# A three-bank score tile that borrows the side work's PSUM bank, and five P buffers for both shapes

## The chip, the cores and the metric

The kernel runs on one core of a Trainium2 chip. The metric is the device time of one execution in microseconds. TensorE (PE) multiplies matrices into PSUM, which has eight banks; ScalarE (ACT) computes the exponentials; VectorE (DVE) and GpSimd (POOL) do elementwise work; SyncE (SP) issues most transfers.

## The reference, cut to what matters

Two identical layers run over x with 2048 rows and 640 columns. Each has an attention block with 32 heads of 20 dimensions and a token-mixing MLP (2048 to 1536 to 2048, along the rows).

```python
x = A_x
x = x + _A_ref(_layernorm(x), A_wqkv, A_wo)                      # attention
x = x + _B_ref(_layernorm(x), B_w1, B_b1, B_w2, B_b2)            # token MLP
x = x + _A_ref(_layernorm(x), A_wqkv, A_wo)
x = x + _B_ref(_layernorm(x), B_w1, B_b1, B_w2, B_b2)

# inside _A_ref, after q, k, v = split(x @ wqkv), H = 32, Dh = 20
scores = jnp.einsum("bhqd,bhkd->bhqk", q, k) * (Dh ** -0.5)
p = _softmax(scores, axis=-1)
o = jnp.einsum("bhqk,bhkd->bhqd", p, v)
```

Per layer that is 2048 x 2048 scores for each of 32 heads, and one exponential for each score.

## The kernel before, in words

**Units, chunks and tiles.** The scores are computed transposed, keys on the 128 partitions. A unit is a group of four heads, a block of 128 keys and a block of 512 queries; it has four chunks, one per head, each 128 keys by 512 queries and as wide as one PSUM bank. A layer has 512 units, 2048 chunks. The loop over t at the end of `attention` goes through score tiles: `take_acts(t)` gathers the next chunks, three where t is even and two where it is odd, `emit_S(t)` (L754) writes the score products of all of them into the tile, and `emit_exp(t)` (L812) has ScalarE turn the whole tile into bf16 probabilities P with one instruction (L818). `emit_PV(n)` (L1418, product at L1440) multiplies the four chunks of a unit with the values and adds them up in the bank `acc`.

**PSUM.** The eight banks are the three-bank score tile, the two-bank score tile, `Dt`, `acc` and `misc`. `misc` is the side work's bank. Side work (fills) are the products that aren't attention itself: projections of queries, keys and values (L1279, L1310), transposes (L1334), the output projection (L1169, L1207) and parts of the token MLP (L1120, L1827). Each group of products fills `misc` and is then evacuated, mostly by VectorE. In the early phase of a layer, before all rows are normalized and projected, `Dt` serves side work too; `feed_ended` closes that phase, opens the pools in the dictionary `late` and takes `Dt` out of the side work's banks.

**Chunks on VectorE.** `ve_admit` (L546) is called once per score tile. Where `Dt` is free and VectorE's backlog is under 7 us, it gives one chunk of a later unit to VectorE: its scores go to `Dt`, and VectorE and GpSimd compute the exponential from bits and a polynomial (L588, L629, L634, L653, L655; L689, L706 on GpSimd). The result is a tile `Pd`.

**P buffers.** P tiles come from two pools of `PT_BUFS` = 3 buffers, one for tiles of three chunks and one for tiles of two. As the shapes alternate, tile t uses the buffer that tile t - 6 had, and ScalarE's write waits until PE has read all of that tile.

**Order of work.** The kernel plans its own order when it is built: PE, DVE, ACT and GpSimd each get a fixed sequence. Clocks for them (`pem`, `dvm`, `acm`) go forward by costs written at the top (`ACT_US`, `WAVE` = 0.2155 us for four products of 512 columns side by side, `ACT_TO_PE` = 0.052 us), and each step asks the clocks what is due. `exp_end[t]` is when ScalarE is planned to finish tile t; scores of tile t + 2 may be written then. `slot_work` (L1496) fills PE's time while an exp runs: a product with the values (`pv_next`, L1459; it is forced once its last tile is `PV_LATE` = 4 tiles back), else side work, else a product with zeros that changes nothing (`zeros`, L775, L807). Side work goes ahead of a waiting product with the values until that is `HOLD` = 3 tiles back. The core of the loop is this:

```python
if not paired and t + 1 not in S_tiles and take_acts(t + 1):
    emit_S(t + 1)
while t - 2 * CFG["PT_BUFS"] in P_tiles:
    slot_work(t, pem["t"] + 0.6, True)
emit_exp(t)
until = exp_end[t] + ACT_TO_PE
while slot_work(t, until):
    ...
```

`P_tiles` holds the tiles that have chunks still to be multiplied. `misc` and `Dbank` (for `Dt`) are objects of the class `Bank`, with `free` as the planned time from which the bank may be used. `next_fill(now)` (L1369) gives the first piece of side work that is ready by then.

Of the kernel before, what the change touches and what calls it, by code (L numbers as in the profile page):

```python
# [12 lines left out]
BF16 = mybir.dt.bfloat16  # L13
F32 = mybir.dt.float32
# [20 lines left out]

CFG = dict(
    KQ_AHEAD=1,
    PT_BUFS=3,
    A0_LAG=2,
    VE_BACKLOG=7.0,  # L40
    VE_MARGIN=3.0,
    VE_LEAST=4,
    PV_LATE=4,
    FILL_ROOM=-0.12,
# [11 lines left out]
ACT_TO_PE = 0.052  # L56
# [16 lines left out]

HOLD = 3
WARM_WAVES = 14
LOG2E = 1.4426950408889634
LN2 = 0.6931471805599453
FIX = 65536.0
# [7 lines left out]
def kernel(  # L86
# [13 lines left out]
    S = A_x.shape[1]  # L100
# [58 lines left out]
    nc.gpsimd.memset(zr[:], 1.0)  # L159
    q_scale = SCALE * LOG2E * FIX  # L160
    x1lp = ctx.enter_context(tc.tile_pool(name="x1lp", bufs=1))
# [12 lines left out]
    def load_w1l():  # L174
        for sti in range(TAIL):
            after_vector(nc.sync.dma_start(out=w1l_view[:, sti, :],
                                           in_=B_w1[(NT - TAIL + sti) * 128:(NT - TAIL + sti + 1) * 128, :]))
# [58 lines left out]

    def open_p_scope(st, stack):
        st.ntmp = stack.enter_context(tc.tile_pool(name=f"ntmp{st.layer}", bufs=1))
        st.ptp = {w: stack.enter_context(tc.tile_pool(name=f"ptp{w}_{st.layer}", bufs=CFG["PT_BUFS"])) for w in (3, 2)}

    def get_QT(st, qb):
        if qb not in st.QTq:
# [3 lines left out]
    def attention(st, x_in_ap, x_mid, uacc_l, feed, feed_stack):  # L246
# [5 lines left out]
        pp = {}  # L252

        def open_psum():
            for name in ("s3", "s2", "dt", "acc", "misc"):
                pp[name] = p1.enter_context(tc.tile_pool(name=f"ps_{name}_{layer}", bufs=1, space=PSUM, reuse_waits="tile"))

        def s_tile(w):
            return pp[f"s{w}"].tile([128, w, 512], F32, name="S")
        ntmp, ptp = st.ntmp, st.ptp  # L260
        p1.enter_context(tc.manual_schedule(engines={nc.vector.engine, nc.scalar.engine, nc.gpsimd.engine}))
        late, ve = {}, {}
# [22 lines left out]
        S_tiles, P_tiles = {}, {}  # L285
        in_attention = [True]

        pem = dict(t=0.0, mode=None)
        dvm = dict(t=0.0, over=DVE_OVER, next=DVE_NEXT, procs=[])
        acm = dict(t=feed.act_free, over=0.0, next=0.06, procs=[])  # L290
# [6 lines left out]
        class Bank:  # L297
            def __init__(self, alloc):
                self.alloc, self.free = alloc, 0.0
        misc = Bank(lambda: pp["misc"].tile([128, 512], F32, name="misc"))  # L300
        Dbank = Bank(lambda: pp["dt"].tile([128, 512], F32, name="Dt"))
        banks = [misc, Dbank]
        spare = [Bank(lambda w=w: s_tile(w)[:, 0, :]) for w in (2, 3)]
# [134 lines left out]
        def unit_ok(u, now):  # L438
            qb, g, _, parts = spans(u)
            return max(max(kready.get(("K", g, p[0] // 4), 1e9) for p in parts), kready.get(("Q", qb, g), 1e9)) <= now + 0.1  # L440
# [58 lines left out]
        def over():  # L499
            return not early[0] and cursor[0] >= NCH  # L500

        def take_acts(t):
            now = pem["t"]
            if not s_start and any(b.free > now for b in spare):
                return []
            acts, c = [], cursor[0]
            while len(acts) < 3 - t % 2:
                n, j = divmod(c, NH)
                if n >= len(units) and not extend(now):
                    break  # L510
                if j == 0 and not unit_ok(units[n], now):
                    break
                c += 1
                if (n, j) not in on_dve:
                    acts.append((n, j))
            ended = not early[0] and c >= NCH
            if len(acts) < 3 - t % 2 and not ended and (not acts or acm["t"] > now + 0.5):
                return []
            for n, j in (divmod(k, NH) for k in range(cursor[0], c)):
                if j == 0:  # L520
                    starts.setdefault(t, []).append(n)
            cursor[0] = c
            for i, (n, j) in enumerate(acts):
                loc[(n, j)] = (t, i)
                last_tile[n] = t
            if acts:
                tile_left[t] = len(acts)
                tiles.append(acts)
            return acts
# [222 lines left out]
        s_start, exp_end = {}, {-2: 0.0, -1: 0.0}  # L752

        def emit_S(t):  # L754
            for n in starts.get(t, ()):
                qb_n, g_n, kt_n = units[n]
                if qb_n > LASTQB and g_n == NG // 2 - 1 and kt_n == 2:
                    load_w1l()
                if qb_n >= 1 and g_n == next_q.get(qb_n, 0) and kt_n == 2 and qb_n + 1 < NQB:
                    enqueue_qproj(qb_n + 1)  # L760
                check_hT_dead()
            w = 3 - t % 2
            St = s_tile(w)
            S_tiles[t] = St
            seen = set()
            dep = exp_end[t - 2] + ACT_TO_PE
            for i, (n, j) in enumerate(tiles[t]):
                s_matmul(St[:, i, :], n, j)
                if not seen or j in seen:
                    s_start[t] = pe_wave("S", dep, cells=cells_s * len(tiles[t]))  # L770
                    seen = set()
                seen.add(j)
            ve_admit(t)
# [38 lines left out]
        def emit_exp(t):  # L812
            St = S_tiles.pop(t)
            ncs = len(tiles[t])
            w = 3 - t % 2
            P = ptp[w].tile([128, w, 512], BF16, name="P")
            P_tiles[t] = P
            nc.scalar.activation(out=P[:, 0:ncs, :].rearrange("p a b -> p (a b)"),  # L818
                                 in_=St[:, 0:ncs, :].rearrange("p a b -> p (a b)"),
                                 func=ACT.Exp, scale=LN2 / FIX)  # L820
            exp_end[t] = max(acm["t"], s_start[t] + PE_TO_ACT - 0.06) + ACT_US[ncs]
            acm["t"] = exp_end[t]

        part_no = {}

# [86 lines left out]
        fs = dict(cur=None, idx=0, tile=None, bank=None)  # L912
# [5 lines left out]
        def check_hT_dead():  # L918
            if not hT_dead[0] and len(kready) == N_KEYS and len(vready) == 2 * NT:
                hT_dead[0] = True  # L920
            return hT_dead[0]
# [369 lines left out]
        def enqueue_qproj(qb):  # L1291
            at = {g: place[(qb, g // 2)] + 8 * (g % 2) if qb == LASTQB else place[(qb, g)]
                  for g in range(NG) if qb == LASTQB or (qb, g) in place}
            if feed.nested:
                late_at = {L: at.pop(L) for L in HIDDEN if L in at}
                for L in late_at:
                    move_queries(L, qb)
                    for p in HIDDEN[L]:
                        if p[0] in at:
                            at[p[0]] = min(at[p[0]], late_at[L])  # L1300
            for g in sorted(at, key=lambda g: at[g]):
                proj_fill("Q", g, qb, at[g] - 10.0, 0.0)
# [66 lines left out]
        def next_fill(now):  # L1369
            held = set()  # L1370
            for grp in fill_queue:
                if grp["key"] in held:
                    continue
                if grp["ready"] <= now and (grp["gate"] is None or grp["gate"]()):
                    return grp
                held.add(grp["key"])
            return None
# [40 lines left out]
        def emit_PV(n):  # L1418
# [16 lines left out]
            for j in range(4):  # L1435
                ti, slot = loc[(n, j)]
                P = ve_P[ti] if (n, j) in on_dve else P_tiles[ti]
                hh_ = 4 * g + j
                for kt, _, w, c0 in parts:
                    pe(nc.tensor.matmul(acc[32 * j:32 * j + 32, a0:a0 + w],  # L1440
                                        lhsT=Vaug[:, (kt * H + hh_) * VW:(kt * H + hh_) * VW + 32],
                                        rhs=P[:, slot, c0:c0 + w], start=(done == 0 and c0 == 0),
                                        stop=final and c0 + w == 512, skip_group_check=True,
# [95 lines left out]
        t = 0  # L1539
        while True:  # L1540
            while t not in S_tiles and not over():
                if take_acts(t):
                    emit_S(t)
                else:
                    slot_work(t - 1, pem["t"] + 0.6, True)
            if t not in S_tiles:
                break
            paired = t % 2 == 1 and t < feed.paired
            if not paired and t + 1 not in S_tiles and take_acts(t + 1):
                emit_S(t + 1)  # L1550
            while t - 2 * CFG["PT_BUFS"] in P_tiles:
                slot_work(t, pem["t"] + 0.6, True)
            emit_exp(t)
            until = exp_end[t] + ACT_TO_PE
# [3 lines that stand above are left out]
            t += 1  # L1558
# [30 lines left out]
        idle = pp["acc"].tile([128, 512], F32, name="acc")  # L1589
        for _ in range(max(4, WARM_WAVES - 4 * rest_fills[0])):  # L1590
            zero_wave(idle, True, True)
# [435 lines left out]
```

## Time and profile before

| | us |
|---|---|
| median of 3 runs | 1738.57 (1737.83 to 1740.37) |
| the profiled execution | 1737.74 |
| its span, first to last instruction | 1736.0 |
| granted TensorE clock, mean | 1.000 |
| ACT busy, of it L818 | 1657.4, 1607.5 |
| DVE busy | 1570.4 |
| PE busy, of it products with zeros into acc (L807) | 1653.5, 346.1 |
| L818 in layer 0, first start to last end | 15.1 to 814.7 |
| L818 in layer 1 | 851.3 to 1666.5 |

A group row of the profile gives the source line, engine and operation, the tile written and the tiles read with their shapes, the number of instructions, busy time and mean length, and after the second bar the time the engine was idle before them with what ended it. In a timeline row the first column is the start and the second the length of a merged stretch.

### The profile page before, as it was taken

The numbers are of one execution on the slowest core, as the hardware profiler recorded it, in microseconds if no ns is written. First come the engines' busy times: TensorE is split into PE (matmuls) and PEld (weight loads), VectorE is DVE, ScalarE is ACT, GpSimd is POOL, SyncE is SP. The second block draws the span as 40 slices with busy tenths as digits, with TensorE's granted clock in tenths as the row PEclk, the third lists the DMA queues.
The fourth block names the chain that finished last, engine by engine and source line by source line (L and its number), as shares of the span: only waits on it lengthen the run. The fifth ranks groups of instructions, "written<-read, shape, count | busy, mean of one in ns | idle before, by whom it ended". The sixth has DMA issues, their size and how long they took to land.

```text
span 1736.0 us, 43779 instructions
## 1 busy us (share of the span) xinstructions
PE 1653.5 (95%) x17971; PEld 662.4 (38%) x18043; DVE 1570.4 (90%) x2547; ACT 1657.4 (95%) x1492; POOL 608.7 (35%) x979
## 2 busy tenths in 40 slices
PE   9999999999999999999999999999999999999999
PEld 3333333333333344444534333333333333444445
DVE  8789999999999999998658869999999999999973
ACT  9999999999999999999789999999999999999970
POOL 3233443443444333343003313334334443434310
PEclk9999999999999999999999999999999999999999
DMA  6000000000112100133322021001002220211245
GB/s 132 14 14 1 1 2 2 23 26 2 35 58 79 48 30 20 40 87 99 117 80 75 25 61 21 6 2 51 18 8 74 83 63 2 83 39 41 70 125 174
DMA packets 105466, 83.88 MB, mean 48 GB/s; under 512 B 52224, under 2 KB 89664, under 8 KB 105264
## 3 DMA queue, kind: packets, MB, share of 16 engines
q1 hardware_dynamic: 99728, 73.19, 14.5%
q0 software_dynamic: 5536, 7.88, 1.5%
q8 instruction: 141, 2.31, 0.6%
q14 instruction: 61, 0.50, 0.1%
HBM read 55.48 MB, written 23.59 MB: 46 GB/s over the span
## 4 chain that ended last, share of the span: by engine, by line
ACT 52%; issue 23%; PE 23%; DVE 1%; DMA 0%; SPq 0%; POOL 0%; another core or an unknown queue 0%; ACTq 0%; DVEq 0%; POOLq 0%
ACT P L818 52%; PE S L748 6%; PE acc L1440 3%; PE ya L1908 2%; PE acc L807 2%; PE misc L1279 2%; PE misc L1120 1%; PE um L1895 1%; PE Dt L1279 1%; PE ya L1917 1%; PE misc L1169 1%; PE yb L1908 1%; PE misc L1827 1%; PE Dt L1827 0%; PE misc L1310 0%
## 5 line engine op out<-in xcount | busy, mean ns | idle before, releaser
L818 ACT ACTIVATE P<-S 128x1536 bf16<-128x1536 f32 (+1 forms) x1421 | 1607.5, 1371 | 9.6 <-PE S L748 9.0
L748 PE MATMUL S<-QTq,KT 32*128 32x512 bf16 (+3 forms) x4429 | 575.1, 336 | 65.6 <-ACT P L818 49.4
L706 POOL TENSOR_SCALAR ey<-ew 128x512 f16<-128x512 uint16 x504 | 313.3, 622 | 620.2 <-DVE ey L634 255.7
L748 PEld LDWEIGHTS <-KT 32*128 32x128 bf16 (+1 forms) x5131 | 231.0, 91 | 521.4 <-issue 492.2
L588 DVE TENSOR_SCALAR ew<-Dt 128x512 int32<-128x512 f32 x522 | 355.3, 681 | 23.1 <-PE Dt L748 16.3
L1440 PE MATMUL acc<-P,Vaug 128*32 128x512 bf16 (+1 forms) x4418 | 365.0, 343 | 0.5 <-issue 0.3
L807 PE MATMUL acc<-zr,zw 128*32 128x512 bf16 x4516 | 346.1, 383 | 1.4 <-POOL zr L159 1.2
L634 DVE SCALAR_TENSOR_TENSOR ey<-ey,ew 128x1024 int16<-128x1024 f16 x261 | 328.7, 1259 | 2.0
L689 POOL TENSOR_SCALAR Pd<-ew 128x512 int16<-128x512 int16 x317 | 195.7, 620 | 232.4 <-DVE ey L634 60.7
L748 PE MATMUL Dt<-QTq,KT 32*128 32x512 bf16 (+3 forms) x702 | 209.8, 334 | 0.0
L629 DVE TENSOR_TENSOR ey<-ey 128x1024 f16<-128x1024 f16 x273 | 196.8, 721 | 2.5 <-POOL ey L706 0.3
L1440 PEld LDWEIGHTS <-Vaug 128*32 128x32 bf16 x5120 | 103.4, 94 | 175.7 <-issue 163.9
L807 PEld LDWEIGHTS <-zw 128*32 128x32 bf16 x4744 | 118.6, 96 | 102.1 <-issue 53.8
L653 DVE TENSOR_TENSOR Pd<-Pd,ey 128x1024 int16<-128x1024 int16 (+1 forms) x197 | 126.7, 643 | 6.3 <-POOL Pd L689 4.6
L655 DVE SCALAR_TENSOR_TENSOR Pd<-ew,ey 128x1024 int16<-128x1024 int16 (+1 forms) x129 | 130.8, 1014 | 0.0
L1440 PE MATMUL acc<-Pd,Vaug 128*32 128x512 bf16 (+1 forms) x702 | 107.2, 337 | 0.0
L948 POOL TENSOR_TENSOR rstd<-veps,mhalf 128x1 f32<-128x1 f32 x60 | 47.7, 796 | 105.9 <-DVE veps L946 81.0
L1120 PEld LDWEIGHTS <-w1st 128*128 128x128 bf16 x672 | 52.4, 97 | 57.1 <-issue 44.9
L1169 PE MATMUL misc<-wo_pad,attnT 128*128 128x320 bf16 x384 | 73.3, 302 | 0.1
L1120 PE MATMUL misc<-x1last,w1st 128*128 128x320 bf16 x384 | 71.6, 302 | 0.0
L855 DVE STREAM_TRANSPOSE T<-acc 128x512 f32<-128x512 f32 (+1 forms) x81 | 56.1, 693 | 9.9 <-PE acc L1440 9.6
L1120 PE MATMUL misc<-hh,w1st 128*128 128x320 bf16 x272 | 49.9, 302 | 0.1
(157 smaller groups left out, 1238.7 us busy)
## 6 DMA issues: line engine op xcount, KB each, us to landing
w2s<-in_B_w_dram SPq DMA_DIRECT2D x16, 768.0 KB
uacc<-ustg POOLq DMA_DIRECT2D x24, 320.0 KB, 2.6
x1in<-xd SPq DMA_DIRECT2D x24, 320.0 KB
w1st<-in_B_w_dram SPq DMA_DIRECT2D x24, 256.0 KB
xd<-x2s SPq DMA_DIRECT2D x16, 320.0 KB
xin<-xd SPq DMA_DIRECT2D x16, 320.0 KB
w1st<-in_B_w_dram SPq DMA_DIRECT2D x21, 192.0 KB
xd<-x1s SPq DMA_DIRECT2D x12, 320.0 KB
```

What stands on the lines that cost most here:

```text
L588: nc.vector.tensor_scalar(out=w[:, slot, :], in0=Dt[:, :], scalar1=127.0 * FIX, scalar2=0.0, op0=ALU.add, op1=ALU.max)
L629: nc.vector.tensor_tensor(out=y, in0=y, in1=y, op=ALU.mult)
L634: nc.vector.scalar_tensor_tensor(out=box["t"][:, 0:512 * k], in0=y[:, 0:512 * k], scalar=MANT_C * MANT_K ** 2, in1=frac, op0=ALU.add, op1= ...
L653: nc.vector.tensor_tensor(out=bits, in0=bits, in1=t, op=ALU.add)
L655: nc.vector.scalar_tensor_tensor(out=bits, in0=whole[:, lo:hi], scalar=128.0, in1=t, op0=ALU.mult, op1=ALU.add)
L689: after_vector(nc.gpsimd.tensor_scalar(out=bits, in0=whole, scalar1=128.0, scalar2=0.0, op0=ALU.mult, op1=ALU.add))
L706: return engine.tensor_scalar(out=out_ap, in0=in_ap, scalar1=MANT_K / FIX, scalar2=-MANT_K * MANT_S, op0=ALU.mult, op1=ALU.add)
L748: pe(nc.tensor.matmul(out_ap[:, c0:c0 + w], lhsT=KT[32 * j:32 * j + feed.rows, g, kt * 128:(kt + 1) * 128], rhs=get_QT(st, qb)[32 * j:32 * ...
L807: pe(nc.tensor.matmul(bank[32 * j:32 * j + 32, 0:w], lhsT=zw[:], rhs=zr[:, :, 0:64].to_broadcast([128, w // 64, 64]), start=start, stop=st ...
L818: nc.scalar.activation(out=P[:, 0:ncs, :].rearrange("p a b -> p (a b)"), in_=St[:, 0:ncs, :].rearrange("p a b -> p (a b)"), func=ACT.Exp, ...
L1120: pe(nc.tensor.matmul(t[:, 0:w], lhsT=w1_of[(p, ft)][:, sti, :], rhs=rows_in[sti][:, c0:c1], start=(sti == 0), stop=(sti == n_in - 1)))
L1440: pe(nc.tensor.matmul(acc[32 * j:32 * j + 32, a0:a0 + w], lhsT=Vaug[:, (kt * H + hh_) * VW:(kt * H + hh_) * VW + 32], rhs=P[:, slot, c0:c0 ...
```

## The change

The two-bank score tile and `misc` become one tile of three banks, `Sm`, of which the side work gets the third bank. An odd tile may be wide: if the early phase is over, no group of side work is in progress, `misc` is free, and no side work is ready now or within `WIDE` = 0.5 us, it takes three chunks, and its scores lie in all three banks of `Sm`. `misc` then counts as taken until the exp of that tile is planned to end. The two P pools become one, with five buffers of three chunks each, for tiles of either size (P takes as much memory as before), and the test ahead of `emit_exp` looks at tile t - 5.

```diff
-    PT_BUFS=3,
+    PT_BUFS=5,
+WIDE = 0.5
-        st.ptp = {w: stack.enter_context(tc.tile_pool(name=f"ptp{w}_{st.layer}", bufs=CFG["PT_BUFS"])) for w in (3, 2)}
+        st.ptp = stack.enter_context(tc.tile_pool(name=f"ptp_{st.layer}", bufs=CFG["PT_BUFS"]))
-            for name in ("s3", "s2", "dt", "acc", "misc"):
+            for name in ("s3", "sm", "dt", "acc"):
-        def s_tile(w):
-            return pp[f"s{w}"].tile([128, w, 512], F32, name="S")
+        def sm():
+            if "three" not in pp:
+                pp["three"] = pp["sm"].tile([128, 3, 512], F32, name="Sm")
+            return pp["three"]
+
+        def s_tile(w, wide=False):
+            if w == 3 and not wide:
+                return pp["s3"].tile([128, 3, 512], F32, name="S")
+            return sm()[:, 0:3 if wide else 2, :]
-        misc = Bank(lambda: pp["misc"].tile([128, 512], F32, name="misc"))
+        misc = Bank(lambda: sm()[:, 2, :])
+        wides = set()
+
+        def wide_now(t):
+            return (t % 2 == 1 and bool(late) and fs["cur"] is None and misc.free <= pem["t"] + 0.02 and
+                    next_fill(pem["t"] + WIDE) is None)
 ...
 def take_acts(t):
+            wide = wide_now(t)
+            most = 3 if wide else 3 - t % 2
 ...
+                if len(acts) > 3 - t % 2:
+                    wides.add(t)
+                    misc.free = 1e9
 ...
 def emit_S(t):
-            w = 3 - t % 2
-            St = s_tile(w)
+            St = s_tile(3 if t in wides else 3 - t % 2, t in wides)
 ...
 def emit_exp(t):
-            P = ptp[w].tile([128, w, 512], BF16, name="P")
+            P = ptp.tile([128, 3, 512], BF16, name="P")
 ...
             acm["t"] = exp_end[t]
+            if t in wides:
+                misc.free = exp_end[t] + ACT_TO_PE
 ...
-            while t - 2 * CFG["PT_BUFS"] in P_tiles:
+            while t - CFG["PT_BUFS"] in P_tiles:
```

More of the change, by code (lines that the diff above doesn't have):

```diff
@@ L506, in take_acts @@
             acts, c = [], cursor[0]
-            while len(acts) < 3 - t % 2:
+            while len(acts) < most:
                 n, j = divmod(c, NH)
@@ L516, in take_acts @@
             ended = not early[0] and c >= NCH
-            if len(acts) < 3 - t % 2 and not ended and (not acts or acm["t"] > now + 0.5):
+            if len(acts) < most and not ended and (not acts or acm["t"] > now + 0.5):
                 return []
@@ L814, in emit_exp @@
             ncs = len(tiles[t])
-            w = 3 - t % 2
-            P = ptp[w].tile([128, w, 512], BF16, name="P")
+            w = 3 if t in wides else 3 - t % 2
+            P = ptp.tile([128, 3, 512], BF16, name="P")
             P_tiles[t] = P
```

## The prediction

> **What bounds the kernel now.** I read the page's busy shares first, then its chain of waits. Exp stands for L818's instruction, chunk for one 128x512 block of scores.
>
> ```profile
> PE 1653.5 (95%) x17971; PEld 662.4 (38%) x18043; DVE 1570.4 (90%) x2547; ACT 1657.4 (95%) x1492; POOL 608.7 (35%) x979
> ...
> ACT 52%; issue 23%; PE 23%; DVE 1%; DMA 0%; SPq 0%; POOL 0%; another core or an unknown queue 0%; ACTq 0%; DVEq 0%; POOLq 0%
> ```
>
> Three engines look full. PE's share holds 346 us of filler products (row L807), so PE has room. The instructions of L818 say whether ScalarE ever rests between two exps:
>
> ```profile
> L818 ACT ACTIVATE P<-S x1421: 653/1286/1716, 15.1 to 1665.4; 128x1536 bf16<-128x1536 f32 x89, 128x1024 bf16<-128x1024 f32 x89
> ...
> its engine sat idle before it (us, times) until:
>   PE S L748: 9.0, 11
>   ACT P L818: 0.2, 1
>   PE acc L1440: 0.2, 1
> ```
>
> It waited 9 us for scores, nearly all at the start of layer 1's attention (854 to 888 us), and 0.2 us, once, for a product that had still to read a P buffer (PE acc L1440). So the two attention stretches last as long as ScalarE's row of exps, and what lengthens or shortens that row changes the time one for one. VectorE, which computes about one chunk in seven, is full too where nothing else is due:
>
> ```profile
> core 0: us, PE busy (x) PEld busy (x) DVE busy (x) ACT busy (x) POOL busy (x), PEclk, DMA share, GB/s
> 585.00:620.00 35.00, 33.45 (x432) 11.60 (x425) 34.02 (x46) 35.00 (x32) 10.97 (x19) 1.00 0.01 2
> 665.00:720.00 55.00, 53.00 (x928) 23.28 (x928) 53.91 (x76) 55.00 (x49) 17.57 (x29) 1.00 0.01 2
> ```
>
> In both windows DVE is busy 97 to 98%, so it won't take more chunks, and longer tiles don't starve it either: it draws 0.43 chunks per us there, while one tile per 1.34 us would offer 0.74.
>
> **Part 1: three chunks where there were two.** By shape the profile has:
>
> ```profile
> L818 ACT ACTIVATE P<-S 128x1536 bf16<-128x1536 f32 x710 | 1123.3, 1582 | 5.7 <-PE S L748 5.0 <-ACT P L818 0.2 <-PE acc L1440 0.2
> L818 ACT ACTIVATE P<-S 128x1024 bf16<-128x1024 f32 x709 | 823.8, 1162 | 3.9 <-PE S L748 3.9
> ```
>
> The means (1.582 and 1.162 us) overlap the neighbour. From the end of one exp to the end of the next the trace has a median of 1.343 us for three chunks and 0.916 us for two: 0.427 us per chunk and 1.343 - 3 x 0.427 = 0.062 us per instruction. Each exp that takes a third chunk saves 1/2.5 of an instruction (a pair now carries 5 chunks), 0.4 x 0.062 = 0.025 us.
>
> How many? Wide tiles exist only with an odd number, after the early phase of each layer (to about 120 us in layer 0 and 1032 us in layer 1, by the last side work on Dt before the layer's tail), with the side bank empty and no side work due. After those times I count 586 exps of two chunks. For each I looked at the moment its scores could be written: in 217 the side bank held nothing and the next side product came over 1.2 us later. Not all will be wide. A wide tile gives its bank back in the plan at exp_end + 0.052, and the next odd tile is chosen at just that moment with a tolerance of 0.02 us, while the planner leaves a slot with 0.01 to 0.06 us to go. I take 6 in 10, so 130 (bounds 100 to 217): 130 x 0.025 = **3.2 us gained** (2.5 to 5.4).
>
> The Trainium skill, ScalarE: Activation LUTs, section What ACT_TABLE_LOAD costs, gives an ACTIVATE 186 ns plus 0.833 ns per element, 93 ns more with a pointer operand, and 93 ns of overlap between neighbours. The slope agrees (0.427 us per 512); its fixed part of up to 187 ns is three times the row's 62. By it the gain would be 130 x 0.4 x 0.187 = 9.7 us. The row decides.
>
> The lent bank keeps side work waiting for up to two exps, 2.7 us, each time a burst begins. That is hidden while bursts are followed by idle stretches, as they are except at the layers' ends, where side work is always due and no tile is wide. The extra score matmul is beside PE's filler. I cost both at nothing; without the cover, see the second rival.
>
> **Part 2: five P buffers for both shapes, in place of three for each.** The bytes are the same (15 chunks), the depth isn't. Exp t now reuses the buffer of tile t-5 where it reused t-6. The trace has no such wait, but has both of its ends: when each exp starts and when the product that reads the last chunk of tile t-5 ends. I went through all exps, counting chunks in order. With six buffers none has to wait by this count. With five, here is one that has to:
>
> ```profile
> 242.59 1.26 ACT L818 ACTIVATE P<-S 128x1024 bf16<-128x1024 f32 x1
> ...
> 242.99 0.39 PE L748 MATMUL S<-QTq,KT 32*128 32x512 bf16 x3 [0.20 <-ACT P L818]
> 243.00 0.39 PE L748 MATMUL Dt<-QTq,KT 32*128 32x512 bf16 x1
> 243.31 0.60 PE L1440 MATMUL acc<-P,Vaug 128*32 128x512 bf16 x5
> ```
>
> The exp at 242.59 would write into the buffer whose last chunk is number 493 of layer 0, and by then 492 had been read. Number 493 is read by the product that starts at 243.31 and ends at 243.70. That product is queued on PE behind the scores of the next tile (242.99), which wait for the previous exp to end (242.93). So with five buffers ScalarE stands still for a score wave, a product and a semaphore. The new loop test ("while t - 5 is in P_tiles, do slot work") emits the late product before the exp, but still behind the next tile's scores, which were emitted just above it, and emit_exp's clock doesn't know the wait, so the plan doesn't avoid it. Behind the exp wait its successors and the scores of t+2; PE runs out of work and DVE is ahead.
>
> An exp may start up to 0.11 us before its predecessor's end without ending later (1419 pairs: the end moves only when the overlap is below that). With 0.05 us for the semaphore the count gives 16 long waits of 0.84 to 1.14 us, 15.2 us, and 72 short ones, 3.0 us: **18.1 us lost** (15.9 us with no semaphore time, 20.0 with 0.07). By place: 1.1 us in layer 0's early phase, 6.1 after it, 6.3 in layer 1's early phase, 4.6 after. The 7.4 us of the early phases come without any wide tile in the plan there. The others lie in bursts of side work, where no tile is wide; after the first wide tile the plan shifts and draws other cases, which I take to be as many, give or take a third (4 us).
>
> **Part 3: layout.** Score tile and side bank are one tile of three banks; Dt and acc move one bank up. At the start of layer 1 Dt lies on a bank that is emptied one row tile later than the plan believes: at most 1 us, once. Below nothing it can't go. I take nothing.
>
> **Sum.** The profiled execution took 1737.74 us (span 1736.0, the rest around it), 0.8 below the median. 1737.7 - 3.2 + 18.1 = 1752.6; on the median **1753**.
>
> **Rivals.** *The five buffers cost nothing.* The plan is redone with the new test, and where products come before the next scores, the wait is gone; this decides if fewer than three of the sixteen long waits stay. Against it: PE's order there is set by the score tile emitted at the top of the step. Then only part 1 is left, 1738.6 - 3.2 = 1735, with 217 wide tiles 1733. Chance 0.14. *The instruction's fixed cost is larger than 62 ns.* At 217 wide tiles and three times the cost the gain is 16 us, and the time 1738.6 + 18.1 - 16 = 1740. Against it stand the ends, constant to 2 ns over 700 pairs. Chance 0.04. The Trainium skill's page named above would have it so. *Lending the bank costs the plan.* Side work starts up to 2.7 us later; what VectorE gets of it arrives in lumps, and chunks that it doesn't take fall to ScalarE at 0.452 us each. If 5% of VectorE's 546 chunks go, 27 x 0.452 = 12 us come on top, 1765; from 30 chunks on it outweighs any wide tile five times. The windows with DVE at 97% speak against it. Chance 0.11. *Wide tiles hardly occur*, if the tolerance of 0.02 us and the side work's look-ahead shut them out: 1738.6 + 18.1 = 1757. Chance 0.06.
>
> **Chances and range.** The forecast has 0.65, and its own range is 1746 (half the 10.7 us of waits outside the early phases gone, all 217 wide: 1738.6 + 12.8 - 5.4) to 1760 (20.0 us of waits and a third more of the late ones, 100 wide). With the rivals, the range that leaves out 2 in 10 (the first rival and the far end of the third) is 1739 to 1766. A measurement of this kernel tells 0.2%, 3.5 us, from no change. Faster by more: most of the first rival, 0.12. Within: the rest of it, and the second rival, 0.08. Slower: 0.80.
>
> **What would show it.** Right: L818's exps fall from 1421 to about 1370, about 815 of 1536 columns; ahead of L818 the idle time that PE acc L1440 ends goes from 0.2 us, once, to 12 to 18 us in some 30 to 80 cases, a third of it between 860 and 1032 us; DVE and PE lose that much busy share; Dt is evacuated about as often as now. Wrong: that row stays under 5 us (the first rival), over 20 chunks move from Dt to L818 (the third), or the exps end other than 1.343 us apart.

## The result and the profile after

The changed kernel takes 2183.83 us (median of 6, 2175.68 to 2194.20) against 1738.66: a ratio of 1.2563, 95% interval 1.2524 to 1.2601. The forecast was 1753, with a range of 1739 to 1766. The direction was right; of the 445 us the forecast had 14. The ratios here and below leave out executions in a slower state, over 1.5% above the fastest of their kernel; two of the four of shared_only were such, and no others.

The page after, busy shares, granted clock and chain, where ScalarE had been busy 95% of the span and half of the chain:

```profile
PE 1851.4 (84%) x18325; PEld 671.3 (31%) x18325; DVE 1582.0 (72%) x2580; ACT 1713.8 (78%) x1449; POOL 603.8 (28%) x968
...
PEclk9889999989889999999979879895775767999999
...
PE 48%; ACT 31%; issue 10%; DVE 10%; DMA 0%; POOL 0%; ACTq 0%; SPq 0%; DVEq 0%
```

No engine is full any more. The chain runs through PE, ScalarE and VectorE in turn, so they wait for each other, and the mean granted clock is 0.881, where it was 1.000. The exps by shape say which of them wait:

```profile
L836 ACT ACTIVATE P<-S 128x1536 bf16<-128x1536 f32 x688 | 1014.6, 1475 | 56.9 <-PE S L767 40.9 <-PE Dt L767 10.0 <-PE acc L1460 3.6
L836 ACT ACTIVATE P<-Sm 128x1024 bf16<-128x1024 f32 x579 | 601.4, 1039 | 343.6 <-PE Sm L1299 43.9 <-PE Sm L1140 38.8 <-PE acc L1460 37.2
L836 ACT ACTIVATE P<-Sm 128x1536 bf16<-128x1536 f32 x108 | 166.5, 1541 | 1.3 <-PE Sm L767 0.9
```

The 108 wide tiles wait 1.3 us in all. The 579 exps of two chunks wait 343.6 us, 0.6 us each, and the first two names of what ends the waits are Sm L1299 and Sm L1140: projections and MLP products, side work in the third bank of the shared tile, which these exps don't read. The instructions of L836 and what ended their waits:

```profile
its engine sat idle before it (us, times) until:
  PE Sm L1299: 45.2, 64
...
  PE Sm L1140: 38.8, 42
  PE Sm L1189: 32.1, 25
  DVE Vaug L403: 23.3, 28
  DVE QTq L405: 22.7, 18
...
who waited for it (us, times):
  PE Sm L767: 91.2, 162
  PE Sm L1299: 43.0, 61
  PE Sm L1140: 39.4, 59
```

Exps wait for VectorE's evacuations of the side bank (Vaug, QTq) too, and side products wait for exps. Before, neither row existed. One round of it, from the timeline (start, length):

```profile
597.57 1.45 ACT L836 ACTIVATE P<-S 128x1536 bf16<-128x1536 f32 x1 [0.50 <-PE Dt L767]
...
598.38 0.55 PE L767 MATMUL Sm<-QTq,KT 32*128 32x512 bf16 x2
...
598.86 0.99 PE L1189 MATMUL Sm<-wo_pad,attnT 128*128 128x320 bf16 x6
...
599.94 1.02 ACT L836 ACTIVATE P<-Sm 128x1024 bf16<-128x1024 f32 x1 [0.92 <-PE Sm L1189]
...
601.02 0.43 PE L1189 MATMUL Sm<-wo_pad,attnT 128*128 128x320 bf16 x2 [0.84 <-ACT P L836]
601.54 0.49 DVE L1201 TENSOR_TENSOR x1s<-Sm,xin 128x320 f32<-128x320 f32 x1 [1.39 <-ACT P L836]
...
602.09 0.39 PE L767 MATMUL Sm<-QTq,KT 32*128 32x512 bf16 x2 [0.64 <-DVE x1s L1201]
...
602.51 1.02 ACT L836 ACTIVATE P<-Sm 128x1024 bf16<-128x1024 f32 x1 [0.20 <-PE Sm L767]
```

The scores were there at 598.93, and ScalarE was free at 599.02. The exp started at 599.94, after six side products that stand between it and its scores in PE's order. The seventh side product then waited for the exp (0.84 us), the evacuation came after that, and the next scores, in banks 0 and 1, waited 0.64 us for an evacuation that reads bank 2.

The program as built says the same. Each exp waits for a value of PE's or VectorE's semaphore, and that value belongs to an instruction:

| exps of two chunks | number | PE wait is for scores | for a side product | for a product with the values | wait for a VectorE evacuation |
|---|---|---|---|---|---|
| before | 709 | 709 | 0 | 0 | 0 |
| after | 579 | 117 | 230 | 76 | 258 |

Of the 579 exps after, the other 156 have no wait of their own for PE, but one for a VectorE evacuation, which itself comes after PE's products. With the side bank as the first of the three banks instead of the last, the built program has the same counts. So the waits don't come from neighbouring banks: in this tile the framework that builds the program makes the later of two instructions on different engines wait for the earlier one, even if both read (an exp and an evacuation) and though they touch different banks. The Trainium skill, PSUM — Partial Sum Buffer, section PSUM bank collisions raise a hardware error, has engines on different banks running without disturbance; the runs below with two tiles in these three banks agree (1740 us with exps and side products side by side). The waits are the program's, not the chip's.

### The profile page after: what moved, and what is told of

The parts are those of the page before. It is cut to its first block, busy times and chain, and to the rows that moved or that the text cites. A ratio compares the mean times of both kernels' runs of the same rounds, so it can differ in the third digit from the quotient of the medians.

```text
span 2192.4 us, 44414 instructions
## 1 busy us (share of the span) xinstructions
PE 1851.4 (84%) x18325; PEld 671.3 (31%) x18325; DVE 1582.0 (72%) x2580; ACT 1713.8 (78%) x1449; POOL 603.8 (28%) x968
## 4 chain that ended last, share of the span: by engine, by line
PE 48%; ACT 31%; issue 10%; DVE 10%; DMA 0%; POOL 0%; ACTq 0%; SPq 0%; DVEq 0%
ACT P L836 31%; PE Sm L767 9%; PE acc L1460 7%; PE Sm L1299 6%; PE Sm L1140 5%; PE acc L825 5%; PE Sm L1189 4%; PE S L767 4%; PE ya L1928 2%; PE Sm L1330 1%; PE Sm L1847 1%; DVE QTq L405 1%; DVE KT L403 1%; PE Dt L1299 1%; DVE Vaug L403 1%
## 5 line engine op out<-in xcount | busy, mean ns | idle before, releaser
L836 ACT ACTIVATE P<-S 128x1536 bf16<-128x1536 f32 x690 | 1016.2, 1473 | 56.9 <-PE S L767 40.9
L836 ACT ACTIVATE P<-Sm 128x1024 bf16<-128x1024 f32 (+1 forms) x688 | 768.5, 1117 | 346.2 <-PE Sm L1299 45.2
L767 PE MATMUL Sm<-QTq,KT 32*128 32x512 bf16 (+3 forms) x1896 | 306.9, 369 | 165.9 <-ACT P L836 91.2
L767 PEld LDWEIGHTS <-KT 32*128 32x128 bf16 (+1 forms) x5201 | 201.5, 92 | 757.3 <-issue 748.8
L1460 PE MATMUL acc<-P,Vaug 128*32 128x512 bf16 (+1 forms) x4418 | 406.2, 379 | 0.9 <-ACT P L836 0.7
L825 PE MATMUL acc<-zr,zw 128*32 128x512 bf16 x4796 | 391.6, 409 | 1.2 <-POOL zr L160 1.2
L767 PE MATMUL S<-QTq,KT 32*128 32x512 bf16 (+3 forms) x2603 | 317.7, 370 | 19.7 <-ACT P L836 17.1
L674 DVE SCALAR_TENSOR_TENSOR Pd<-ew,ey 128x512 int16<-128x512 int16 (+1 forms) x136 | 128.6, 946 | 0.0
L1189 PE MATMUL Sm<-wo_pad,attnT 128*128 128x320 bf16 x384 | 93.8, 373 | 25.4 <-ACT P L836 25.2
L1140 PE MATMUL Sm<-x1last,w1st 128*128 128x320 bf16 x384 | 85.8, 349 | 26.4 <-ACT P L836 26.2
L1140 PEld LDWEIGHTS <-w1st 128*128 128x128 bf16 x672 | 60.4, 103 | 106.4 <-issue 88.7
```

The costliest lines, as they stand in the source:

```text
L767: pe(nc.tensor.matmul(out_ap[:, c0:c0 + w], lhsT=KT[32 * j:32 * j + feed.rows, g, kt * 128:(kt + 1) * 128], rhs=get_QT(st, qb)[32 * j:32 * ...
L825: pe(nc.tensor.matmul(bank[32 * j:32 * j + 32, 0:w], lhsT=zw[:], rhs=zr[:, :, 0:64].to_broadcast([128, w // 64, 64]), start=start, stop=st ...
L1140: pe(nc.tensor.matmul(t[:, 0:w], lhsT=w1_of[(p, ft)][:, sti, :], rhs=rows_in[sti][:, c0:c1], start=(sti == 0), stop=(sti == n_in - 1)))
L1189: pe(nc.tensor.matmul(t[:, 0:w], lhsT=attnT[g][:, ttl * 128:(ttl + 1) * 128], rhs=wo_pad[:, g, c0:c1], start=(g == 0), stop=(g == NG - 1)))
L1460: pe(nc.tensor.matmul(acc[32 * j:32 * j + 32, a0:a0 + w], lhsT=Vaug[:, (kt * H + hh_) * VW:(kt * H + hh_) * VW + 32], rhs=P[:, slot, c0:c0 ...
```

## The experiments

**Three theories.** A: the shared tile's waits are the cause; the prediction's two other terms hold besides. B: the P buffers are. C: lending the bank to wide tiles is.

**p5_only**: the kernel before with the P pools alone changed.

```diff
-    PT_BUFS=3,
+    PT_BUFS=5,
 ...
-        st.ptp = {w: ... bufs=CFG["PT_BUFS"])) for w in (3, 2)}
+        st.ptp = stack.enter_context(tc.tile_pool(name=f"ptp_{st.layer}", bufs=CFG["PT_BUFS"]))
 ...
-            P = ptp[w].tile([128, w, 512], BF16, name="P")
+            P = ptp.tile([128, 3, 512], BF16, name="P")
 ...
-            while t - 2 * CFG["PT_BUFS"] in P_tiles:
+            while t - CFG["PT_BUFS"] in P_tiles:
```

> The kernel before with the P pools alone changed: one pool of five three-chunk buffers, the test at t - 5; PSUM as before, no wide tile. Theory A (the shared score-and-side tile makes its readers and writers wait for each other): this kernel has none of that, so only the P waits counted before are left, 1738.7 + 18 = 1757 (1750 to 1762), clock 1.00, idle time ahead of the exps ended by PE acc about 15 us in 30 to 90 cases. Theory B (P buffers are the cause of the whole loss): over 2000. Theory C (lending the bank to wide tiles is the cause): also 1757.

Measured: 1773.23 us, ratio 1.0204 (1.0178 to 1.0231). B falls. The 1750 to 1762 that A and C named is missed too: the term is larger than the forecast's 18 us, as is told with the prediction's part 2 below.

**shared_only**: the kernel before with the PSUM layout alone changed.

```diff
-            for name in ("s3", "s2", "dt", "acc", "misc"):
+            for name in ("s3", "sm", "dt", "acc"):
 ... (sm() as in the change)
-            return pp[f"s{w}"].tile([128, w, 512], F32, name="S")
+            if w == 3:
+                return pp["s3"].tile([128, 3, 512], F32, name="S")
+            return sm()[:, 0:2, :]
 ...
-        misc = Bank(lambda: pp["misc"].tile([128, 512], F32, name="misc"))
+        misc = Bank(lambda: sm()[:, 2, :])
```

> The kernel before with the PSUM layout alone changed: the two-bank score tile and the side bank are slices of one three-bank tile; no wide tile, P pools as before. Theory A: the false waits alone cost nearly everything, 2120 to 2190, clock 0.87 to 0.92, 300 us or more of idle time ahead of exps that read Sm. Theory B and theory C: 1739, clock 1.00.

Measured: 2174.61 us (median of 4, 2148.34 to 2188.38), ratio 1.2408 (1.2351 to 1.2465), which is some 418 us more than before, clock 0.893 in the profiled execution. A holds, C falls: no tile is wide here. Its exps by shape, in the same view as above:

```profile
L825 ACT ACTIVATE P<-S 128x1536 bf16<-128x1536 f32 x710 | 1044.0, 1470 | 59.3 <-PE S L755 38.8 <-PE Dt L755 18.5
L825 ACT ACTIVATE P<-Sm 128x1024 bf16<-128x1024 f32 x709 | 741.8, 1046 | 315.5 <-PE Sm L1127 49.4 <-PE Sm L1286 41.5 <-PE Sm L1176 31.7
```

**nowide**: the changed kernel with `wide = False` in `take_acts`.

> The changed kernel with the wide tiles switched off (wide = False in take_acts): shared tile and five buffers stay. Theory A: within 30 us of the changed kernel, 2150 to 2215, rather the upper half since the exps of 108 wide tiles are the only ones on Sm that never wait for side work. Theory B: the same as the changed kernel within 5 us. Theory C: 1757.

Measured: 2191.45 us, ratio 1.2614 (1.2583 to 1.2644). As A says; B named the same number, but had fallen with p5_only.

**split_p5**: the changed kernel with the three banks handed between two layouts. Dt and acc come from the other end of PSUM, so that these three can be closed and opened.

```diff
+        def region(names):
+            if now_open["names"] == names:
+                return
+            if now_open["stack"] is not None:
+                now_open["stack"].close()
+            now_open.update(names=names, stack=ExitStack() if names else None)
+            for name in names or ():
+                ps_pool(now_open["stack"], name)
+        def misc_tile():
+            region(("s2", "misc"))
+            return pp["misc"].tile([128, 512], F32, name="misc")
 ...
 def s_tile(w, wide=False):
-            return sm()[:, 0:3 if wide else 2, :]
+            region(("w3",) if wide else ("s2", "misc"))
+            return pp["w3" if wide else "s2"].tile([128, 3 if wide else 2, 512], F32, ...)
```

> The changed kernel with the score tile and the side bank as two tiles again while no tile is wide: the three banks belong either to a pool for the two-bank score tile and one for the side bank, or to one pool for the three-bank tile, and are handed over when a wide tile begins or ends; 108 wide tiles and five P buffers stay. Theory A: the forecast of the prediction comes true here, 1753 (1746 to 1760), clock 1.00. Theory B and theory C: 2150 or more.

Measured: 1762.42 us, ratio 1.0145 (1.0128 to 1.0162), clock 1.00. The change without the shared tile is what the prediction had forecast, 2 us outside its own range. What ends the waits of its exps:

```profile
L852 ACT ACTIVATE P<-S 128x1536 bf16<-128x1536 f32 x688 | 1061.1, 1542 | 7.8 <-PE S L783 6.8 <-PE acc L1476 0.5
L852 ACT ACTIVATE P<-S 128x1024 bf16<-128x1024 f32 x580 | 645.0, 1112 | 20.0 <-PE acc L1476 15.9 <-PE S L783 4.0
L852 ACT ACTIVATE P<-Sw 128x1536 bf16<-128x1536 f32 x108 | 171.7, 1590 | 0.0
```

343.6 us have become 20.0, and 15.9 of them are the P waits.

**dep_both, dep_exp, dep_pe**: the kernel before, with the waits and without the shared tile. `hold` adds a dependency on an earlier instruction by its name; `side` keeps the names of the last side product, evacuation and odd exp.

```diff
 # emit_exp, t odd                      (dep_exp and dep_both)
+                hold(inst.ins, side["product"])
+                hold(inst.ins, side["evac"])
 # fill_step, bank is misc; emit_S, t odd  (dep_pe and dep_both)
+                hold(nc.cur_bb.bb.instructions[-1], side["exp"])      # side product
+                        hold(made, side["exp"])                       # its evacuation
+                    hold(nc.cur_bb.bb.instructions[-1], side["evac"]) # scores
```

> The kernel before, every tile and bank where it was, with waits added by hand as the shared tile would make them: the exp of an odd tile waits for the last side product into misc and its evacuation that were issued ahead of it; each side product into misc and its evacuation wait for the last such exp; the scores of an odd tile wait for the last evacuation of misc. If the waits are the whole cause, this alone is as slow as the shared tile: 2120 to 2200, clock 0.87 to 0.91. If it is where the banks lie, or anything else in the shared tile, 1739.

> The same with the first kind of wait alone: exps of odd tiles wait for side products and their evacuations, PE and VectorE are free. If ScalarE's waits carry the loss, since ScalarE bounds the kernel: 2000 to 2150. If the loss needs the ring in which each waits for the other: 1780 to 1900.

> The same with the other kinds alone: side products and evacuations wait for the last exp of an odd tile, the scores of odd tiles for the last evacuation; exps wait for nothing new. If ScalarE's waits carry the loss: 1745 to 1800. If PE's waits, by which the scores that ScalarE needs come late, carry it: 2000 to 2150.

Measured, one execution each beside 1738.78: 2164.30, 1890.57 and 1866.72 us. The waits alone make the loss: 425.5 us, where the shared tile alone lost some 418. Neither kind makes it by itself (151.8 and 127.9 us, 280 together). The other 146 us appear only with both kinds, where a ring is closed: an exp waits for side products that wait for the last exp. How much of them is the lower clock (0.887, against 0.979 and 0.969 with one kind) was not separated. So the second answer of dep_exp is right, and dep_pe was expected wrongly on both sides.

**split_ring**: split_p5 with P in one tile of 15 chunks, used as a ring.

```diff
-    PT_BUFS=5,
+    PT_CHUNKS=15,
 ...
+        P_ring = ptp.tile([128, CFG["PT_CHUNKS"], 512], BF16, name="P")
+        def P_room(t):
+            n = len(tiles[t])
+            lo = P_at[t - 1][1] if t else 0
+            if lo + n > CFG["PT_CHUNKS"]:
+                lo = 0
+            P_at[t] = (lo, lo + n)
+            return [q for q in P_tiles if P_at[q][0] < lo + n and lo < P_at[q][1]]
 ...
-            while t - CFG["PT_BUFS"] in P_tiles:
+            while P_room(t):
```

> The split kernel (two tiles or one, handed over; 108 wide tiles) with P in one ring of 15 chunks, 2 or 3 of them per tile, in place of five buffers: six tiles deep while 3 and 2 alternate, five while all are wide, at the same bytes. In the built program 27 exps wait for a product with the values, 178 with five buffers and 16 before. If the P waits are all that the split kernel lost: 1738.5 - 2.7 = 1736 (1733 to 1740), faster than both. If wide tiles cost something of their own: 1745 to 1760.

Measured: 1741.32 us, ratio 1.0012 (1.0003 to 1.0021). The P waits are gone (0.5 us left ahead of the exps), and with them 21 of the 24 us that split_p5 lost. Neither answer is met, and it isn't faster than before: its exps need 2.7 us less (their lengths summed at 1.343, 0.916 and 0.489 us: 1601.3 against 1604.0), but 1.9 us went into the stretch between the layers' exps (38.5 against 36.5), 1.5 into waits in the first 50 us of layer 1 and 1.8 into waits in layer 0. One tile of 15 chunks is read and written here by two engines at once, and in the built program 27 of 1378 exps wait for a product with the values: in this SBUF tile the framework looks at the part that is touched.

**ring_banks** and **ring_tol**: the ring kernel with the banks renamed, and that with more wide tiles.

```diff
-  yb0, ya0, ya1, yb1 = (... for name in ("yb0", "ya0", "ya1", "yb1"))
+  yb0, yb1, ya0, ya1 = (... for name in ("yb0", "yb1", "ya0", "ya1"))   # both
-            return (... misc.free <= pem["t"] + 0.02 and
+            return (... misc.free <= pem["t"] + 0.07 and                  # ring_tol
```

> The ring kernel with the banks of layer 1's opening products named in the order yb0, yb1, ya0, ya1, so that Dt, acc and the side bank follow the same product as in the kernel before. The ring kernel lost 1.9 us between the two layers' exps and 1.4 us in the first 50 us of layer 1 against before. If the bank order is the cause of these: 1738.0 (1736.5 to 1739.5), the gap between the layers' exps back at 36.5 us. If not: 1741.

> The same, and the planner's tolerance for the lent bank goes from 0.02 to 0.07 us, so that a wide tile can follow a wide tile: 178 wide tiles in place of 108. At 0.025 us per wide tile 1.7 us less than the kernel with the bank order alone: 1736.3 (1734.5 to 1738). If wide tiles in a row delay side work or VectorE's chunks: 1739 or more.

Measured: 1740.04 us, ratio 1.0005 (0.9996 to 1.0013), and 1739.01 us, ratio 0.9996 (0.9987 to 1.0005), beside 1739.67 for before. Neither can be told from before, and neither of the gains that were expected shows. In ring_banks the start of layer 1 is as before again (7.9 us of waits in its first 50 us, 7.8 before; 9.3 in split_ring and in ring_tol), the gap between the layers isn't (38.2 and 38.1 us): its cause is open. With 178 wide tiles the exps need 3.5 us less than before (1600.4 against 1604.0), and that is about as much as the rest costs.

**p5_floor** and **after_floor**: more products with zeros.

```diff
-    FLOOR=(0.52, 0.48),
-    FLOOR_RUN=(0.68, 0.64),
+    FLOOR=(0.72, 0.68),
+    FLOOR_RUN=(0.88, 0.84),
```

> The kernel with five P buffers alone (p5_only), with the planner's floor of PE work raised (FLOOR from 0.52, 0.48 to 0.72, 0.68; FLOOR_RUN from 0.68, 0.64 to 0.88, 0.84), which puts some 830 more products with zeros into PE's idle time. If the 12 us that p5_only lost around 1205 to 1232 us, where the granted clock was 0.52, came from PE having too little to do while ScalarE waited: clock 1.00 throughout, no such stretch, 1757 to 1763. If that stretch has another cause: 1768 to 1780 again.

> The changed kernel with the same raised floor. If the lowered clock (0.88) makes a large part of its loss: clock over 0.93 and 2050 to 2130. If the waits alone make it, or if zeros can't help because PE stands behind its own waits: 2170 to 2210, clock as before.

Measured: 1779.08 us, ratio 1.0239 (1.0214 to 1.0264), and 2168.56 us, ratio 1.2450 (1.2415 to 1.2486), clock 0.896 in the profiled execution. Filler doesn't mend it. In p5_floor the slow stretch at 1205 us is gone, but the clock is halved from 1415.0 to 1435.5 us (and at 36 and 992 us, for 6.8 us each), and exps lose 15.7 us in layer 0, where p5_only lost 9.4. A filler that stands in PE's order ahead of what ScalarE waits for may make that late; no run shows how much. How much of the changed kernel's loss is the clock was not settled. In its six executions the time went with the clock, 2175.68 us at 0.892 to 2194.20 at 0.881; carried on in a straight line to 1.0 that is 1989 us, so some 195 of the 445 us. That is an estimate far outside its data, and as the waits also leave PE idle, it doesn't separate the two.

## Why the prediction was wrong

**Part 3, layout, is the step that failed.** "I take nothing" and "Below nothing it can't go" were said of where the banks lie. No run has the changed kernel's own places without the shared tile; with other places the ring kernels come within 3 us of before. What was missed is that a tile is the unit by which the program waits in PSUM. The prediction went through who frees which bank and didn't ask whether two slices of one tile are two things to the framework that places the semaphores; it assumed the waits of before, bank by bank. That term, put at nothing, measured some 418 us alone (shared_only) and 425.5 with the waits alone (dep_both).

**The third rival, which part 1 calls the second, priced lending the bank, not sharing the tile.** Lending costs little: with wide tiles off, the changed kernel is no faster (nowide), and VectorE evacuates Dt for its own chunks as often as before (522 times). The claim that side work's lateness is hidden fits ring_banks and ring_tol, which can't be told from before.

**Part 1 was right in kind and size.** 108 wide tiles for 130; in the ring kernels three-chunk exps end 1.343 us apart and two-chunk exps 0.916; 2.7 us gained by these lengths where 3.2 were forecast. No kernel came out faster than before by it. The 62 ns per instruction held, and so the Trainium skill's fixed part of up to 187 ns, weighed against it there, doesn't fit here.

**Part 2 was right wait by wait and a third to a half too small in sum.** The long waits came where the count had put them. The exp of the example waits in p5_only:

```profile
245.78 3.28 ACT L818 ACTIVATE P<-S 128x1024 bf16<-128x1024 f32 x3 [0.86 <-PE acc L1440]
```

It ends 0.97 us late (0.93 in the count). All sixteen exps for which the count had a long wait have one in p5_only, and fourteen of these are within 0.15 us of the count. The other two, counted at 1.14 and 0.92 us, are 2.74 and 2.62 us late, and both lie in one stretch that the count couldn't have. The windows are us, then busy time and number of instructions of PE, weight loads, DVE, ACT and POOL, then the clock:

```profile
1196.70:1200.40 3.70, 2.56 (x30) 0.81 (x27) 2.74 (x5) 3.13 (x3) 1.24 (x2) 1.00 0.03 6
1200.50:1231.10 30.60, 28.61 (x153) 7.26 (x152) 18.07 (x31) 19.69 (x18) 9.41 (x15) 0.50 0.10 33
1231.30:1255.00 23.70, 22.26 (x196) 7.97 (x194) 23.50 (x42) 23.70 (x22) 12.42 (x19) 1.00 0.25 75
```

From 1200.5 to 1231.2 us PE's clock was halved, a score product took 0.61 us instead of 0.39, and scores and products with the values came late:

```profile
1203.82 0.62 PE L1440 MATMUL acc<-P,Vaug 128*32 128x512 bf16 x4
...
1204.52 3.35 ACT L818 ACTIVATE P<-S 128x1024 bf16<-128x1024 f32 x3 [2.63 <-PE acc L1440]
```

Against before, p5_only's exps lose 31.7 us more in its profiled execution, and 12.2 of these lie in that stretch. With its two counted waits at their counted length, and without a wait of 1.4 us that falls into 3.4 us of halved clock at 893 us, some 20 us are left, the upper end of the 15.9 to 20.0 of the prediction. The prediction says that PE runs out of work behind such a wait; what its sum lacked is that the clock can fall. What made it fall is open. A wait of 0.97 us had ended 3 us before, but thirteen others like it at full clock had no halving within 5 us behind them.

The Trainium skill, TensorE: Matmul & The Clock Gate, section What's actually happening, lets the array's clock fall to one half after an idle window of about 3.4 us. The trace agrees with the half, and its two halvings before the end, 3.41 and 30.72 us long, are one and nine times 3.41 us. But PE was busy 2.56 of the last 3.7 us at full clock, and its longest rest there was 0.95 us, so no idle stretch of that length came before.

With six buffers, where the prediction says that no exp has to wait, its count with 0.05 us for the semaphore gives fifteen short waits, 0.6 us together.

**What would show it.** The number of exps came out near the forecast in the changed kernel and in split_p5 alike (1378, 796 of them of 1536 columns). The other sign, 12 to 18 us of exps waiting for PE acc, is there in split_p5 (16.4 us, in 21 cases where 30 to 80 were named); the changed kernel has 40.8 us of it in 45. No sign on the list looked at exps that wait for side work.

## What to carry to other kernels

Before two buffers are merged into slices of one tile, look in the built program at what each reader waits for: in PSUM the framework ordered the accesses of PE, ScalarE and VectorE to one tile, reads against reads included, and that cost 24% here, while the same three banks as two tiles cost nothing that could be told from before. If one region must serve two shapes, hand it over between pools. And where an order of work is planned ahead, count for every shared buffer when it would be free against when it would be taken: that count found the 16 long waits one by one in the trace of before, though not what the clock made of two of them.

## What was not expected of the hardware

In p5_only PE's clock was halved for 30.7 us, although PE was busy 2.56 of the 3.7 us before that and 28.61 of the 30.6 us in it. Executions of a kernel with many waits differ by more than those of before: the changed kernel 2175.68 to 2194.20 us, at clocks of 0.892 to 0.881, before 1737.83 to 1740.37 in the same comparison.
